# Third channel chunk of a dense convolution on TensorE: computed twice, or once and copied across partition halves

## The chip, the cores and the metric

The kernel runs on one core of one Trainium2 chip. The metric is the device time of one execution in microseconds (us). The core has five engines, each with its own queue: TensorE (PE, its weight loads shown as PEld), VectorE (DVE), ScalarE (ACT), GpSimd (POOL) and SyncE (SP, which here only issues DMAs). They work side by side and wait for each other through semaphores. TensorE writes its results into PSUM, eight banks of 128 partitions x 512 float32; ACT or DVE copy them out to SBUF. Such a copy is called an eviction here.

## The reference, cut to what matters

Eight sequences of 4160 tokens, 192 channels, eight heads of 24 channels. Each head has seven taps; they are put through a softmax and used as a causal convolution along the tokens. The result goes token by token into a maxout layer and an output product.

```python
w = softmax(weight)                                   # 8 heads x 7 taps
out = np.einsum('hk,bskhg->bshg', w, x_unf)           # y[s] = sum over k of w[h,k] * x[s - 6 + k]
x = out.reshape(B * S, D)                             # 33280 x 192
h = np.maximum(np.maximum(x @ w1, x @ w2), x @ w3)    # 192 -> 768
return (h @ w_out).astype(np.float32)                 # 768 -> 192
```

The kernel computes the maxout as max(relu(y(w1-w3)), y(w2-w3)) and adds y(w3 w_out) to the last product, so the third first-layer product is never made per token.

## The kernel before, in words

The tokens are worked on in 65 blocks of 512. The 192 channels are three chunks of 64. The first layer's operands have channels on partitions, 64 to a half, so that two 64-row products run on the two halves of the array: one half makes lp (w1-w3), the other lq (w2-w3). The convolved input therefore has to lie on both halves.

Blocks 4 to 64 get their convolution in token order (`conv`, L354), are transposed by DMA, and POOL copies them to the other half (`double`). The first four blocks, which open the kernel, use the dense conv (`conv_dense`, L376), which gives channels on partitions directly. It multiplies slots of 32 channels of x (tile xz, stationary, 32 columns wide) with a band matrix of the taps. A block is five chunks of at most 103 tokens; a slot of 32 channels can span two heads, so each product is made from two versions v of xz, which are added in PSUM. Four slots at a time go to four column groups of the array, that is to partitions 0, 32, 64 and 96 of the result.

For n = 0 these are slots 0 to 3, the first two channel chunks: PSUM tile D0, evicted to `yd[:, 0, :]`. `cross` (L395) copies each half of that to the other half. For n = 1 they are slots 4, 5, 4, 5: the third channel chunk made twice, once for each partition half, in PSUM tile D1, evicted in one copy to `yd[:, 2, :]`. In blocks 0 and 1 the crossing is done on the weights instead of the data (`cross_wd`, L322).

The order of the work is written out by hand: each engine runs its instructions in the order in which the program issues them. The steps around the change are, in this order (L692 to L741):

- `conv_dense(0)`: D0 evicted by ACT, D1 by DVE. Behind it: on ACT a zeroing of part of the input buffer of block 6 (`zero_x`, L140) and half of the casts of block 1 (`cast_dense`, L216); on DVE `copy_w3` (L316) and `make_wd` (L312). POOL makes the other half of the casts. The first-layer products of block 0 that need D0 (F) come on PE behind the conv.
- `conv_dense(1)` in the order n = 1, then n = 0: D1 evicted by ACT, D0 by DVE. On PE the products of block 0 that need its third chunk (H), then those of block 1 (H, F) in the pool psw, whose four buffers the four D tiles held before; these products of block 1 are the tiles lw. On DVE two `make_wd` and the first h of block 0.
- The rest of the first layer of blocks 0 and 1, a transposition of w3 on PE (`transpose_w3`, tiles pt), and the second layer of block 0 without its y part (`first_hidden`, L613).
- `conv_dense(2)`: D0 evicted by ACT, D1 by DVE, and then `cross` with ACT and DVE (L399). On PE `make_m` (L347), which multiplies w3 and w_out into the tiles pm0 and pm1; ACT evicts them (L349). Two zeroings (ACT L140, DVE L137). The pool psp, from which pm0, pm1 and then the lp of the main loop come, has two buffers.
- The main loop, block 2 first. It issues the first layer of a block (`l1`, L517) interleaved with the second layer of the block before (`st2`, L582); ACT makes r = relu(lp) (L500), DVE h = max(r, lq) (L505), ACT and DVE together add up two halves of the output (L589, L590).
- In block 2, behind its second first-layer tile, `conv_dense(3)`: D0 by ACT, D1 by DVE, a zeroing by DVE (L137), `cross` on POOL, the load and casts of later blocks.

SP's queue holds the loads of x and the stores and transposes, in program order. The loads of blocks 7 and 8 wait for zeroings of the buffers that they go to.

Of the kernel before, what the change touches and what calls it, by code (L numbers as in the profile page):

```python
# [19 lines left out]
GRP = 24  # L20
BAND_W = 128 + PAD
NBLK = 512
CHK = 103
HALF = P // 2
# [4 lines left out]
def kernel(  # L29
# [12 lines left out]
    nc = tc.nc  # L42
# [15 lines left out]
    for b in range(B):  # L58
        s = nfull * NBLK
        while s < SEQ:  # L60
            n = min(SEQ - s, NBLK - off)
# [13 lines left out]
    def conv_chunks(blk):  # L75
        res = []
        for (b, S, N, off) in blk:
            for o_lo in range(0, N, CHK):
                o_hi = min(o_lo + CHK, N)
                row_lo = max(0, S + o_lo - PAD)  # L80
                rlen = min(16 * ceil((CHK + PAD) / 16), SEQ - row_lo)
                res.append((len(res), b, row_lo, rlen, off + o_lo, off + o_hi,
                            o_lo - (row_lo - S)))
        return res

    NDENSE = 4
    chunks_of = [conv_chunks(blk) for blk in blocks[:NDENSE]]
    NQ = len(chunks_of[0])
# [42 lines left out]
    def zero_x(t, q0=0, q1=NR, eng=None):  # L131

        if t >= NDENSE:
            get_x(t)
        xf = xbuf[t]
        if eng is not None:
            eng.memset(xf[TOK:HALF, q0:q1, :], 0.0)  # L137
            return
        zero = idle[TOK:HALF, 0:D]
        nc.scalar.copy(out=xf[TOK:HALF, q0:q1, :],  # L140
                       in_=bass.AP(tensor=zero.tensor, offset=zero.offset,
                                   ap=[list(zero.ap[0]), [0, q1 - q0], [1, D]]))
# [43 lines left out]
    def cast_x(t):  # L186
        if not 0 <= t < NB:
            return
        xf, p0, _ = xin.pop(t)
        t0, u, nu = place(t)  # L190
        if u == 0:
            pool = x16q if nu >= 4 else x16p
            x16 = pool.tile([P, NHEAD * 4 * 2 * GRP * (5 if nu >= 4 else nu)], FP16, tag="x16", name=f"x16_{t0}")
            x16s[t0] = x16[:, 0:NHEAD * 4 * 2 * GRP * nu].rearrange("p (h j u r c) -> p h j u r c", h=NHEAD, j=4, u=nu, r=2)
        if p0:
            nc.gpsimd.memset(xf[0:p0, 0, :], 0.0)
        K = HALF + KR
        for r in range(2):
            nc.gpsimd.tensor_copy(out=x16s[t0][0:K, :, :, u, r, :].rearrange("p h j c -> p j h c"),  # L199
                                  in_=xf[0:K, 4 * r:4 * r + 4, :].rearrange("p j (h c) -> p j h c", c=GRP))  # L200
# [3 lines left out]
    xz = {t: [const.tile([P, NQ, D], FP16, name=f"xz_{t}_{v}") for v in range(2)] for t in range(2)}  # L204
# [72 lines left out]
    band = bands[:, 0:NHEAD * BAND_W].rearrange("p (h w) -> p h w", w=BAND_W)  # L277
# [11 lines left out]
    for lo, hi, copy in ((0, CUT, nc.scalar.copy), (CUT, WIN, nc.vector.tensor_copy)):  # L289
        bps = psq.tile([32, hi - lo + 3, NHEAD], FP32, tag="q", name=f"band_{lo}")  # L290
        for c in range(lo, hi):

            nc.tensor.matmul(bps[:, c - lo:c - lo + 4, :].rearrange("p c h -> p (c h)"),
                             lhsT=line[:, WIN - 1 - c:WIN + 31 - c],
                             rhs=ident16[:, 0:4 * NHEAD], start=True, stop=True)
        for a in range(4):
            copy(out=band[32 * a:32 * a + 32, :, 32 * a + lo:32 * a + hi],
                 in_=bps[:, 0:hi - lo, :].rearrange("p c h -> p h c"))
# [11 lines left out]
    def make_wd(n, j0, j1, eng=nc.vector):  # L310
        f = slice(P * j0, P * j1)
        eng.tensor_sub(out=wd[:, n, f], in0=ws[:, n, f], in1=w3s[:, n // 2, f])  # L312
# [5 lines left out]
    def cast_w3(j0, j1):  # L318
        f = slice(P * j0, P * j1)
        nc.gpsimd.tensor_copy(out=w3h[:, :, f], in_=w3s[:, :, f])  # L320
# [52 lines left out]
            slots[t0] = ysp.tile([P, 2, nu, 2, D], FP16, tag="ys", name=f"ys_{t}")  # L373
        convs[t0] = G, heads[0]

    def conv_dense(t, copies, pools=((None, None),) * 2, order=(0, 1)):  # L376


        yd = dense[t] = ydp.tile([P, NC, NBLK], FP16, tag="yd", name=f"yd_{t}")
        for n in order:  # L380
            slots_ = ((0, 1, 2, 3), (4, 5, 4, 5))[n]
            pool, tag = pools[n]
            ps = (pool or psw).tile([P, NBLK], FP32, tag=tag or "w", name=f"D{n}_{t}")
            for (q, b, row_lo, rlen, lo, hi, cc) in chunks_of[t]:
                for v in range(2):
                    for g, s in enumerate(slots_):
                        h = (32 * s + 31 * v) // GRP
                        nc.tensor.matmul(  # L388
                            ps[32 * g:32 * g + 32, lo:hi],
                            lhsT=xz[t][v][0:rlen, q, 32 * s:32 * s + 32],  # L390
                            rhs=band[0:rlen, h, cc:cc + hi - lo],
                            start=(v == 0), stop=(v == 1), tile_position=(0, 32 * g))
            copies[n](out=yd[:, 2 * n, :], in_=ps[:])

    def cross(t, *copies):  # L395

# [27 lines left out]
    def double(t):  # L424

        if not NDENSE <= t < NB:
            return
        yp = dense[t]
        for i in range(2):
            nc.gpsimd.tensor_copy(out=yp[HALF * i:HALF * (i + 1), 1, :, :, :, :].rearrange("p i u k n -> p (i u k n)"),  # L430
                                  in_=yp[HALF * (1 - i):HALF * (2 - i), 0, :, :, :, :].rearrange("p i u k n -> p (i u k n)"))
# [35 lines left out]
    def op(fn):  # L467
        ops.append((tuple(put), fn))
# [137 lines left out]
    def first_hidden(k):  # L606

        meet()
        first.append(psw.tile([P, 2, D], FP32, tag="w", name=f"po_0_{k}"))
        for s in range(2):  # L610
            for j in range(NJ):
                n = 2 * k + s
                nc.tensor.matmul(first[k][:, s, :], lhsT=hs[0][:, j, P * n:P * (n + 1)], rhs=wo[:, j, :],  # L613
                                 start=(s == 0 and j == 0), stop=False)
# [72 lines left out]
    PQ = ((psp, "p"), (psq, "q"))  # L687
    WW = ((psw, "w"), (psw, "w"))
    WPWQ = ((psw, "w"), (psp, "p"), (psw, "w"), (psq, "q"))
    ACT, DVE = nc.scalar.copy, nc.vector.tensor_copy  # L690
    GP = nc.gpsimd.tensor_copy
    make_wd(0, 0, 2)  # L692
    make_wd(1, 0, 2)
    zero_x(6, 4, NR, nc.vector)
    conv_dense(0, (ACT, DVE))
    zero_x(6, 0, 4)
    for t in range(NDENSE, XBUF):
        load_x(t)
# [7 lines left out]
    for n in range(NC):  # L706
        make_wd(n, 4, 6, nc.gpsimd)
    cast_w3(2, 6)
    conv_dense(1, (DVE, ACT), order=(1, 0))
    make_wd(0, 2, 4)  # L710
    make_wd(1, 2, 4)
    cross_wd(0, GP)
# [16 lines left out]
    cross_wd(1, ACT)  # L729
    first_hidden(0)  # L730
    first_hidden(1)
    conv_dense(2, (ACT, DVE), (WW[0], PQ[1]))
    cast_x(4)
    cross(2, ACT, DVE)
    make_m(0)
# [26 lines left out]
    for t in range(2, NB):  # L762
        u = convs_at.get(t, NB)
        late = t > 2 and u < NB
        if t in (3, 4):
            double(t + 1)
        if t > 3:
            for v in range(casts.get(t - 1, 8) + 1, casts[t] + 1):
                cast_x(v)
        l1(t, 0)  # L770
        if t == 2:
            first_rest()
        elif t == 3:
            cast_x(8)
            nc.gpsimd.tensor_copy(out=m16[0:HALF, 2, :], in_=m16[HALF:P, 0, :])
            nc.gpsimd.tensor_copy(out=m16[HALF:P, 2, :], in_=m16[HALF:P, 1, :])
        if t > 3 and not late:
            op(lambda t=t: (store(t - 2, 0, 4, (nc.sync,)),
                            turn(t + 2, (2,)) if place(t + 2)[1:] in ((0, 4), (0, 5)) else None,
                            turn(t + 1, (4,)) if place(t + 1)[1:] == (0, 5) else None, load_on(t)))  # L780
        else:
            op(lambda t=t: store(t - 2, 0, 4, (nc.sync,)))
        cuts = ROOM if late else EVEN
        st2(t - 1, (cuts[0], cuts[0]))
        for j in range(1, NJ):
            l1(t, j)
            if late and j == 1:
                st2(t - 1, (cuts[0] + OWN + AHEAD, cuts[0] + OWN))
                meet()
                quad, second = u >= QUADS, u < QUADS or t == u - 3  # L790
                conv(u, WPWQ, range(4 * second, 4 * second + 4) if quad else range(NHEAD))
                for i in (0, 2):
                    evac(u, i)
                for i in (1, 3):
                    evac(u, i, nc.vector.tensor_copy)
                if second:
                    turn(u)
                load_on(t)
            if t == 2 and j == 1:
                meet()  # L800
                conv_dense(3, (ACT, DVE))
                zero_x(1, NQ, NR, nc.vector)
                cross(3, GP, GP)
                load_x(8)
                cast_x(6)
            elif t == 2 and j == 3:
                meet()
                conv(u, WW)
                evac(u, 0)
                evac(u, 1, nc.vector.tensor_copy)  # L810
                turn(4)
                load_x(9)
                cast_x(7)
            st2(t - 1, (cuts[j], cuts[j]))
            if j == 1 and t > 4 and t + 2 in pairs and pairs[t + 2][1] % 2 == 0:
                double(t + 2)
            if t == NB - 1 and j == 3:
                op(lambda: store(NB - 2, 0, 2, (nc.sync,)))
        if t == NB - 1:
            op(lambda: store(NB - 2, 2, 4, (nc.sync,)))  # L820
# [29 lines left out]
```

## Time and profile before

| what | value |
|---|---|
| median of 3 runs | 453.1 us (452.54 to 453.47) |
| profiled execution | 452.5 us, span 450.7 us |
| PE busy | 444.7 us, 99% of the span |
| DVE / ACT / POOL busy | 356.5 / 320.3 / 204.0 us |
| DMA | 72.01 MB, mean 160 GB/s |
| dense conv matmuls (L388) | 320, from 6.2 to 27.2 us, 205 to 221 ns each, overlapping |
| evictions of D (L393) | 4 by ACT, 586 ns; 4 by DVE, 684 to 692 ns |

The span runs from the first to the last instruction of the profiled execution; all times in a timeline are us from its start. A line of the timeline gives the start, the duration, the engine, the line of the kernel, the operation, the output and input tiles with partitions x elements, how many instructions it merges, and in brackets the idle time of that engine just before and what ended it. The duration of a merged line runs from the first start to the last end. Matmuls overlap, so the sum of their durations is no time on the engine. In the groups by shape the columns behind the bar are the busy time in us, the mean duration in ns, and the idle time in front.

### The profile page before, as it was taken

What the parts mean: (1) busy time and instruction counts of PE and PEld (TensorE: products, weight loads), DVE (VectorE), ACT (ScalarE), POOL (GpSimd) and SP (SyncE); (2) the same over time, 40 slices, a digit from 0 to 9 for tenths busy, and PEclk for the clock granted to TensorE, in tenths of its full rate; (3) what the DMA queues carried; (4) which work ended last, traced back from release to release, by engine and by line L of the source; (5) the groups of instructions that cost most, each with busy time, mean ns of one, the idle gap of its engine ahead of it and who ended that gap; (6) DMA issues with size and microseconds to landing.
All of it is one profiled execution on the core that took longest, in us unless ns stands there. A gap on an engine that the chain in (4) does not pass through costs nothing.

```text
span 450.7 us, 18261 instructions
## 1 busy us (share of the span) xinstructions
PE 444.7 (99%) x7576; PEld 409.5 (91%) x7576; DVE 356.5 (79%) x610; ACT 320.3 (71%) x600; POOL 204.0 (45%) x234
## 2 busy tenths in 40 slices
PE   7999999999999999999999999999999999999997
PEld 4579999999999999999999999999999999999996
DVE  7778778878778787787887887887887887887775
ACT  7977677767677676776776777776776776776664
POOL 2874836556464524714724635526544545124000
PEclk9999999999999999999999999999999999999999
DMA  7978999495977759649559749769549566172123
GB/s 204 238 191 158 208 183 240 134 217 148 183 208 161 184 107 214 172 112 205 158 138 185 190 103 193 192 105 218 157 116 207 160 157 151 48 139 75 56 71 106
DMA packets 128242, 72.01 MB, mean 160 GB/s; under 512 B 52320, under 2 KB 127967, under 8 KB 128159
## 3 DMA queue, kind: packets, MB, share of 16 engines
q1 hardware_dynamic: 127999, 70.75, 68.8%
q8 instruction: 59, 0.97, 1.0%
q14 instruction: 24, 0.20, 0.2%
q10 hardware_dynamic: 160, 0.10, 0.1%
HBM read 33.28 MB, written 25.56 MB: 131 GB/s over the span
## 4 chain that ended last, share of the span: by engine, by line
PE 97%; DMA 1%; SPq 1%; issue 0%; DVE 0%; POOL 0%; POOLq 0%
PE po L582 36%; PE lq L517 32%; PE lp L517 22%; PE G L367 3%; PE lw L541 1%; DMA xf<-in_x_dram 1%; PE D L388 1%; PE lp L541 1%; PE po L613 0%; PE po L640 0%; SPq L233 0%; SPq L229 0%; PE pm L347 0%; PE lq L541 0%; SPq L167 0%; PE pt L338 0%
## 5 line engine op out<-in xcount | busy, mean ns | idle before, releaser
L582 PE MATMUL po<-wo,h 64*128 64x192 f16 x3024 | 331.7, 243 | 0.0
L505 DVE TENSOR_TENSOR h<-r,lq 128x512 f16<-128x512 f16 x384 | 263.0, 686 | 84.3 <-ACT r L500 74.3
L500 ACT ACTIVATE r<-lp 128x512 f16<-128x512 f32 x384 | 229.0, 597 | 113.4 <-PE lp L517 103.0
L517 PE MATMUL lp<-yp,wd 64*128 64x512 f16 x1098 | 295.6, 376 | 0.0
L517 PE MATMUL lq<-yp,wd 64*128 64x512 f16 x1098 | 295.5, 376 | 0.0
L582 PEld LDWEIGHTS <-h 64*128 64x128 f16 x3024 | 242.6, 94 | 5.5 <-issue 4.1
L517 PEld LDWEIGHTS <-wd 64*128 64x128 f16 x2268 | 181.6, 94 | 14.9 <-issue 0.2
L199 POOL CAST x<-xf 103x768 f16<-103x768 f32 x122 | 97.2, 825 | 112.4 <-DMA xf<-in_x_dram 108.9
L582 PE MATMUL po<-m,yp 64*128 64x192 f16 x720 | 140.3, 243 | 0.0
L430 POOL COPY yp<-yp 64x1536 f16<-64x1536 f16 (+1 forms) x70 | 90.9, 1298 | 87.3 <-DMA yp<-ys 62.3
L590 DVE TENSOR_TENSOR o<-a,po 128x384 f32<-128x384 f32 x126 | 69.0, 548 | 0.0
L582 PEld LDWEIGHTS <-yp 64*128 64x128 f16 x720 | 66.3, 94 | 0.1
L589 ACT COPY a<-po 128x384 f32<-128x384 f32 x126 | 59.5, 472 | 0.0
L407 ACT CAST ys<-G 128x480 f16<-128x480 f32 (+1 forms) x53 | 25.4, 530 | 9.5 <-PE G L367 9.5
L407 DVE CAST ys<-G 128x480 f16<-128x480 f32 (+1 forms) x53 | 30.2, 610 | 0.0
L367 PE MATMUL G<-x,band 39*32 39x240 f16 (+3 forms) x1024 | 16.5, 242 | 0.0
L367 PEld LDWEIGHTS <-band 39*32 39x32 f16 x1024 | 10.2, 91 | 4.6 <-issue 4.1
L517 PE MATMUL lq<-yd,wd 64*128 64x512 f16 x36 | 9.7, 376 | 0.0
L517 PE MATMUL lp<-yd,wd 64*128 64x512 f16 x36 | 9.7, 376 | 0.0
L541 PEld LDWEIGHTS <-wd 128*128 128x128 f16 (+1 forms) x48 | 3.1, 96 | 6.0 <-issue 2.8
L216 POOL CAST xz<-xf 112x160 f16<-112x160 f32 (+2 forms) x15 | 4.3, 330 | 7.9 <-DMA xf<-in_x_dram 7.8
L388 PEld LDWEIGHTS <-xz 112*32 112x32 f16 x320 | 3.9, 96 | 2.7 <-POOL xz L216 1.1
(79 smaller groups left out, 98.1 us busy)
## 6 DMA issues: line engine op xcount, KB each, us to landing
xf<-in_x_dram SPq DMA_DIRECT2D x113, 234.0 KB
out_dram<-o SPq DMA_DIRECT2D x62, 384.0 KB
wall<-in_moe_w_dram SPq DMA_DIRECT2D x12, 128.0 KB
xf<-in_x_dram SPq DMA_DIRECT2D x7, 204.8 KB
xf<-in_x_dram SPq DMA_DIRECT2D x3, 420.0 KB
yp<-ys SPq DMA_TRANSPOSE x70
out_dram<-o SPq DMA_DIRECT2D x5, 192.0 KB
wos<-in_moe_w_out_dram SPq DMA_DIRECT2D x1, 576.0 KB
```

The lines of the kernel that those rows point to most:

```text
L199: nc.gpsimd.tensor_copy(out=x16s[t0][0:K, :, :, u, r, :].rearrange("p h j c -> p j h c"), in_=xf[0:K, 4 * r:4 * r + 4, :].rearrange("p j ( ...
L367: nc.tensor.matmul(G[2 * (k // per) + i][TOK * j:TOK * (j + 1), k % per, :], lhsT=band[row, h, HALF * i + LAP:HALF * i + KR], rhs=x16s[t0] ...
L388: nc.tensor.matmul(ps[32 * g:32 * g + 32, lo:hi], lhsT=xz[t][v][0:rlen, q, 32 * s:32 * s + 32], rhs=band[0:rlen, h, cc:cc + hi - lo], star ...
L407: copy(out=slots[t][:, i % 2, :, :, GRP * h0:GRP * (h0 + per)].rearrange("p u r (h c) -> p h (u r) c", c=GRP), in_=G[i][:].rearrange("p h ...
L430: nc.gpsimd.tensor_copy(out=yp[HALF * i:HALF * (i + 1), 1, :, :, :, :].rearrange("p i u k n -> p (i u k n)"), in_=yp[HALF * (1 - i):HALF * ...
L500: nc.scalar.activation(out=r[:], in_=ps[0][:], func=AF.Relu)
L505: nc.vector.tensor_max(out=hs[t][:, j, :], in0=r[:], in1=q[:])
L517: nc.tensor.matmul(ps[i][:], lhsT=w_of(i, c, j), rhs=y_all(t, i, c), start=(n == 0), stop=(n == NC - 1))
L541: nc.tensor.matmul(open_ps[t, j, i][:], lhsT=a, rhs=b, start=(t, j, i) not in begun, stop=(t, j, i) in begun)
L582: nc.tensor.matmul(ps[b0, i][:, s % 2, :], lhsT=a, rhs=b, start=first, stop=last)
L589: nc.scalar.copy(out=a[:], in_=ps[s - 1, 0][:])
L590: nc.vector.tensor_add(out=outs[t][:, s - 1:s + 1, :], in0=a[:], in1=ps[s - 1, 1][:])
```

## The change

For n = 1 only two slots are multiplied per token chunk, 4 and 5, once. The five token chunks are dealt over the halves of the result: chunks 0, 1 and 2 (tokens 0 to 308) go to column groups 0 and 1 (partitions 0 to 63), chunks 3 and 4 (tokens 309 to 511) to groups 2 and 3 (partitions 64 to 127). They are issued in units of two token chunks, 0 with 3 and 1 with 4, and chunk 2 alone. The third chunk takes 20 matmuls instead of 40.

Each half of D1 then holds other tokens, and each has to reach both halves of `yd[:, 2, :]`. So the one eviction of 128 x 512 becomes four: tokens 0 to 308 of 64 partitions, to their own half and to the other one, by `copies[1]`, and tokens 309 to 511 in the same way by `copies[2]`. The argument `dup` would make the second copy from SBUF; no call gives it. Conv 0, 2 and 3 have DVE and ACT as these engines, conv 1 ACT and DVE.

```diff
-    def conv_dense(t, copies, pools=((None, None),) * 2, order=(0, 1)):
+    def conv_dense(t, copies, pools=((None, None),) * 2, order=(0, 1), dup=None):
         yd = dense[t] = ydp.tile([P, NC, NBLK], FP16, tag="yd", name=f"yd_{t}")
+        ch = chunks_of[t]
+        FAR = (NQ + 1) // 2
         for n in order:
-            slots_ = ((0, 1, 2, 3), (4, 5, 4, 5))[n]
+            if n == 0:
+                units = [[(c, 0, (0, 1, 2, 3))] for c in ch]
+            else:
+                units = [[(c, 2 * (c[0] // FAR), (4, 5)) for c in ch[k::FAR]] for k in range(FAR)]
             pool, tag = pools[n]
             ps = (pool or psw).tile([P, NBLK], FP32, tag=tag or "w", name=f"D{n}_{t}")
-            for (q, b, row_lo, rlen, lo, hi, cc) in chunks_of[t]:
+            for unit in units:
                 for v in range(2):
-                    for g, s in enumerate(slots_):
-                        h = (32 * s + 31 * v) // GRP
-                        nc.tensor.matmul(
...
+                    for (q, b, row_lo, rlen, lo, hi, cc), g0, slots_ in unit:
+                        for g, s in enumerate(slots_, g0):
+                            h = (32 * s + 31 * v) // GRP
+                            nc.tensor.matmul(
...
-            copies[n](out=yd[:, 2 * n, :], in_=ps[:])
+            if n == 0:
+                copies[0](out=yd[:, 0, :], in_=ps[:])
+            else:
+                far = ch[FAR][4]
+                for i, (lo, hi) in enumerate(((0, far), (far, NBLK))):
+                    own, other = (slice(HALF * k, HALF * (k + 1)) for k in (i, 1 - i))
+                    copies[1 + i](out=yd[own, 2, lo:hi], in_=ps[own, lo:hi])
+                    if dup is None:
+                        copies[1 + i](out=yd[other, 2, lo:hi], in_=ps[own, lo:hi])
+                    else:
+                        dup(out=yd[other, 2, lo:hi], in_=yd[own, 2, lo:hi])
...
-    conv_dense(0, (ACT, DVE))
+    conv_dense(0, (ACT, DVE, ACT))
...
-    conv_dense(1, (DVE, ACT), order=(1, 0))
+    conv_dense(1, (DVE, ACT, DVE), order=(1, 0))
...
-    conv_dense(2, (ACT, DVE), (WW[0], PQ[1]))
+    conv_dense(2, (ACT, DVE, ACT), (WW[0], PQ[1]))
...
-                conv_dense(3, (ACT, DVE))
+                conv_dense(3, (ACT, DVE, ACT))
```

More of the change, by code (lines that the diff above doesn't have):

```diff
@@ L382, in conv_dense @@
             pool, tag = pools[n]
             ps = (pool or psw).tile([P, NBLK], FP32, tag=tag or "w", name=f"D{n}_{t}")
-            for (q, b, row_lo, rlen, lo, hi, cc) in chunks_of[t]:
+            for unit in units:
                 for v in range(2):
-                    for g, s in enumerate(slots_):
-                        h = (32 * s + 31 * v) // GRP
[L388 to L392, printed above, removed]
@@ L393, in conv_dense @@
-            copies[n](out=yd[:, 2 * n, :], in_=ps[:])
+                    for (q, b, row_lo, rlen, lo, hi, cc), g0, slots_ in unit:
+                        for g, s in enumerate(slots_, g0):
+                            h = (32 * s + 31 * v) // GRP
+                            nc.tensor.matmul(
+                                ps[32 * g:32 * g + 32, lo:hi],
+                                lhsT=xz[t][v][0:rlen, q, 32 * s:32 * s + 32],
+                                rhs=band[0:rlen, h, cc:cc + hi - lo],
+                                start=(v == 0), stop=(v == 1), tile_position=(0, 32 * g))
```

## The prediction

> **What bounds the kernel now.** I read the page's busy table and the chain that ended last, then the timeline of the stretch in which the dense conv runs, engine by engine, and last the groups by shape for durations.
>
> ```profile
> PE 444.7 (99%) x7576; PEld 409.5 (91%) x7576; DVE 356.5 (79%) x610; ACT 320.3 (71%) x600; POOL 204.0 (45%) x234
> ...
> PE 97%; DMA 1%; SPq 1%; issue 0%; DVE 0%; POOL 0%; POOLq 0%
> ```
>
> TensorE is busy from end to end at a granted clock of 9 tenths or more, and 97% of the chain is its own. So from about 12 us on, what PE gains or loses reaches the end, unless a wait for ACT or DVE takes it up. The dense conv (L388) runs four times, all before 28 us: PE starts it at 6.22, 9.87, 21.61 and 26.34. I call them conv 0 to 3. Each is 80 matmuls in 1.10 us (1.30 in conv 1, which waits for its casts). First ACT around conv 2:
>
> ```profile
> 22.32 0.59 ACT L393 CAST yd<-D 128x512 f16<-128x512 f32 x1
> 22.93 0.62 ACT L399 COPY yd<-yd 64x512 f16<-64x512 f16 x1
> 23.46 0.71 ACT L349 CAST m<-pm 128x192 f16<-128x192 f32 x2
> 24.20 0.67 ACT L140 CAST xf<-idle 32x576 f32<-32x576 f16 x1
> 24.89 0.60 ACT L500 ACTIVATE r<-lp 128x512 f16<-128x512 f32 x1
> 25.39 0.47 ACT L629 COPY o<-po 128x384 f32<-128x384 f32 x1
> ```
>
> ACT has no gap here. PE in the same stretch:
>
> ```profile
> 21.61 1.10 PE L388 MATMUL D<-band,xz 112*32 112x103 f16 x80
> 22.65 1.16 PE L347 MATMUL pm<-wo,w3t 128*128 128x192 f16 x12
> 23.81 0.37 PE L517 MATMUL lp<-yd,wd 64*128 64x512 f16 x1
> ```
>
> Pool psp has two buffers and pm0 and pm1 hold them, so the first lp of block 2 takes pm0's and waits for ACT's eviction of it (L349). That ends at 23.46 + 0.31 = 23.77, and lp starts at 23.81: PE and ACT arrive together, with no slack.
>
> Conv 1, all engines:
>
> ```profile
> 10.75 0.59 ACT L393 CAST yd<-D 128x512 f16<-128x512 f32 x1 [0.54 <-PE D L388]
> ...
> 11.23 0.69 DVE L393 CAST yd<-D 128x512 f16<-128x512 f32 x1 [1.59 <-PE D L388]
> ...
> 12.27 1.19 PEld L541 LDWEIGHTS <-wd 128*128 128x128 f16 x7 [0.63 <-issue]
> ```
>
> The weight load at 12.27 stood idle 0.63 us, against 0.42 at this place of the next two rounds. The lw of block 1 in front of it takes D0's PSUM buffer, and DVE frees that at 11.23 + 0.69 = 11.92: DVE's eviction, not PE, sets this place.
>
> Conv 3, on DVE:
>
> ```profile
> 27.67 0.68 DVE L393 CAST yd<-D 128x512 f16<-128x512 f32 x1
> 28.53 0.54 DVE L137 MEMSET xf<- 32x576 f32 x1 [0.17 <-issue]
> 29.27 0.69 DVE L505 TENSOR_TENSOR h<-r,lq 128x512 f16<-128x512 f16 x1 [0.20 <-ACT r L500]
> 29.88 0.55 DVE L590 TENSOR_TENSOR o<-a,po 128x384 f32<-128x384 f32 x1
> ```
>
> L590 ends at 30.43 and frees a po buffer; PE's weight load at 30.48 has idled 0.19 for it. DVE's own idle time between its conv 3 eviction and there is only 0.17 + 0.20.
>
> Rows for the new shapes, by shape, on ACT, then DVE:
>
> ```profile
> L349 ACT CAST m<-pm 128x192 f16<-128x192 f32 x2 | 0.6, 313 | 0.1
> ...
> L629 ACT COPY o<-po 128x384 f32<-128x384 f32 x1 | 0.5, 473 | 0.0
> ```
>
> ```profile
> L629 DVE COPY o<-po 128x384 f32<-128x384 f32 x1 | 0.6, 552 | 0.0
> ```
>
> **The change, part by part.**
>
> *Matmuls.* Four 32-column matmuls on different column groups run beside each other: 80 in 1.03 to 1.10 us is 20 sets of 51 to 55 ns. The third chunk had 5 token chunks x 2 versions = 10 sets; it becomes units (chunks 0+3, 1+4, 2) x 2 versions = 6 sets, the last two half filled. Four sets less: 4 x 52 = 0.21 us per conv. If the cost goes by instruction, 20 x 13.4 ns = 0.27; if two token chunks don't run beside each other, 0. I take 0.21, as PE already runs four different right sides at once.
>
> *Evictions.* One 128x512 copy per conv (DVE 0.69; ACT 0.59 in conv 1) becomes two 64x309 on one engine and two 64x203 on the other. By the line through 313 ns at 192 elements and 473 at 384, ACT takes 0.32 for 203 and 0.41 for 309. DVE's 552 at 384 and 690 at 512 give 1.08 ns per element: 0.47 for 309, 0.36 for 203. Half the partitions shorten nothing: the 64x512 copies (L399) take 0.62 and 0.58. Bounds are the rows on either side: on ACT 0.31 to 0.47, on DVE 0.23 (32x80, L297) to 0.69.
>
> *How closely they follow.* Some neighbours on ACT overlap: 24.89 + 0.60 is 25.49, and the next starts at 25.39. Others don't: 22.32 + 0.59 = 22.91 and 22.93; the band copies out of PSUM into one quarter of the partitions after the other (L297, 0.334 each) take 1.02 for three. On DVE two L505 take 1.28 against 2 x 0.685, but the full-height eviction of 22.77 (0.69) and the copy across halves at 23.49 don't overlap. The new pieces change halves at each step, so I take the rows without overlap for both engines: 0.02 between pieces. [...]
>
> *Conv 0.* PE ends long before ACT (7.60) and DVE (8.17) evict; later it idles 0.91 for D0, unchanged, and then for the casts of block 1. Its 0.21 is hidden: 0. On ACT the two pieces delay the zeroing (8.21, L140) by 0.68, to 8.89 to 9.72. Behind it stand ACT's casts of block 1: at 9.74 instead of 9.44. DVE's third chunk ends at 9.13 for 8.86; copy_w3 and make_wd behind it end near 9.9 and first serve at 11.1: 0.
>
> *Conv 1.* PE's second unit needs ACT's second cast, ready at 10.41 instead of 10.11; five of six sets follow, so the third chunk ends near 10.8 (10.75 before) and D0's near 11.34 (11.23). ACT: 10.82 + 0.41 + 0.02 + 0.41 = 11.66, for lw at 11.62: 0.1 late. DVE, new here, takes two pieces to 11.49, and only then D0: 11.51 to 12.20 instead of 11.92. So lw is 0.28 late; behind D0 on DVE are two make_wd and the first h, all 0.28 later, and PE wants them in turn. POOL's wd, which held PE's weights 0.05 at 14.15, takes back 0.05. Loss 0.23. Ends: a gain of 0.2 if the casts are on time and DVE's pieces are at 0.31; a loss of 0.5 at 0.47 each.
>
> *Conv 2* (times before shifts). PE ends 0.21 sooner, pm too (23.60). DVE: 22.56 + 0.47 + 0.02 + 0.47 = 23.52, its crossing copy from 23.49 to 23.54: 0. ACT: D0 22.32 to 22.91, pieces 22.93 and 23.27, crossing copy 23.61 to 24.23, pm0 24.25 to 24.56. So lp starts at 24.61 for 23.81: loss 0.80, PE's 0.21 swallowed. Behind on ACT: pm1, the zeroing (24.80 to 25.47), r of block 2 (25.49; its lp is ready 25.42), L629, which frees the buffer that conv 3 wants 0.8 later too: all in time. SP's load of block 7 waits for that zeroing, 0.6 later, less than PE's own delay: 0. Ends: pieces hidden, a gain of 0.21; both at 0.47, a loss of 1.1.
>
> *Conv 3.* ACT idles 1.02 before 28.64, which covers its 0.68. DVE takes 0.96 for 0.69: the memset slides to 28.80, h from 29.27 to 29.36, L590 ends at 30.52. PE, 0.21 sooner, waits for it: loss 0.09 (ends: gain 0.2, loss 0.4). POOL's crossing copies wait for D0 alone, and SP's load of block 8, behind that memset (now 29.07), has its cast at 38.14; the transposes queued behind that load on SP start at 30.85, 0.6 after it, which covers 0.27. No DMA is added. After 31 us all is as before, shifted.
>
> *Sum.* 0 + 0.23 + 0.80 + 0.09 = +1.1 us on the profiled execution's 452.5 us (span 450.7, 1.8 around it): 453.6. That execution stands 0.6 below the median of 453.1, so I forecast 454.2 for the median.
>
> **The rivals.** (1) *ACT's pieces overlap*, by 0.10 as at 25.39. Then conv 0's casts start on time (9.44), conv 1 loses nothing, and in conv 2 the pieces start at 22.82 and 23.05, pm0 ends at 24.12, lp at 24.17: loss 0.36. With conv 3: +0.4, 453.5. For it: the crossing copy of 22.93 overlaps pm by 0.09 across halves. Against: L297's three.
> (2) *PE's time counts*: ACT's pieces come in front of pm0 for nothing. For it: the chain is 97% PE. Against: ACT's full row from 22.32 on. Conv 2 and 3 gain 0.21 each, conv 1 up to 0.2: 452.5 to 452.7; at 0.27 each 452.3. It needs lp before 23.81, and is faster by 0.2% only beyond 0.27 each, since conv 0 is hidden.
> (3) *Two token chunks don't run together*, so PE saves nothing. The third chunk of conv 1 ends at 11.0, and DVE's D0 at 12.4: +0.45; conv 2 the same 0.80, conv 3 0.2: 454.5.
>
> **How the numbers follow.** A measurement of this kernel can tell about 0.2%, 0.9 us (its runs lie 452.54 to 453.47). Chances: my sum 0.50, rival 1 0.20, rival 2 0.10, rival 3 0.10, something not seen 0.10. Slower (over 454.0): 0.30 of my sum, which lies only 0.2 above the bound, 0.08 of rival 3, 0.03 of rival 1, 0.06 unseen: 0.47. Faster (under 452.2): 0.03 of rival 2, 0.02 unseen: 0.05. Within: 0.48. The range is 452.7 to 455.2: from rival 2's less favourable end to my sum with each ACT and DVE piece at its upper row.
>
> **What would show it.** Right: L388 near 0.9 us in conv 2; ACT's L393-like pieces near 0.32 with gaps of 0.02; its casts of block 1 near 9.74; D0 of conv 1 evicted near 11.5; lp of block 2 at 24.6 plus 0.23, PE idle in front. Wrong: lp near 24.2 and casts at 9.44 (rival 1); lp at 23.6 (rival 2); L388 still 1.1 (rival 3). A piece far from its line, or a new wait after 31 us, would break the sum.

## The result, and the profile after

The changed kernel takes 458.47 us (median of 6 runs, 457.36 to 460.04) against 452.82 us before (6 runs, 452.47 to 455.06): 1.19% slower by the ratio of the means, 1.0119, with a 95% interval of 1.0091 to 1.0146. The forecast was 454.2. The profiled execution took 457.36 us with a span of 455.6, 4.9 more than the 450.7 before. From its page, the busy table and the shares of the chain that ended last:

```profile
PE 445.7 (98%) x7496; PEld 408.9 (90%) x7496; DVE 357.6 (78%) x615; ACT 322.4 (71%) x607; POOL 204.1 (45%) x234
...
PE 95%; DVE 2%; ACT 1%; issue 1%; ACTq 0%; DVEq 0%
```

The new copies add 2 us to ACT's busy time and 1 to DVE's, far less than 4.9. The chain shows more: DVE, ACT and "issue" now hold 4% of it, where they held nothing. The totals of the waits between 8 and 36 us name the new ones:

```profile
DVE yd L405 <- ACT yd L407: 2.9, 1, 2.9
ACT yd L405 <- DVE yd L407: 2.1, 2, 1.1
...
PE lp L533 <- ACT m L349: 1.7, 1, 1.7
```

L405 and L407 are the new pieces: L405 the copy to a half's own partitions, L407 that to the other half. The first piece of the engine that comes second waits for the other engine's last one. (Of DVE's 2.9 in conv 1 only the last 0.88 is this wait: D1 was complete by 11.84, when ACT began on it, and DVE started at 12.72.) Conv 2 on ACT, the timeline:

```profile
24.96 0.59 ACT L400 CAST yd<-D 128x512 f16<-128x512 f32 x1
26.26 0.32 ACT L405 CAST yd<-D 64x203 f16<-64x203 f32 x1 [0.71 <-PE pm L347]
26.59 0.33 ACT L407 CAST yd<-D 64x203 f16<-64x203 f32 x1
26.94 0.62 ACT L415 COPY yd<-yd 64x512 f16<-64x512 f16 x1
27.58 0.54 ACT L349 CAST m<-pm 128x192 f16<-128x192 f32 x2
```

and on DVE:

```profile
25.19 0.47 DVE L405 CAST yd<-D 64x309 f16<-64x309 f32 x1 [2.11 <-PE D L394]
25.70 0.47 DVE L407 CAST yd<-D 64x309 f16<-64x309 f32 x1
26.09 0.40 DVE L415 COPY yd<-yd 64x512 f16<-64x512 f16 x1
```

ACT is free at 25.55 and D1 complete before 25.19, yet ACT's first piece starts at 26.26, just after DVE's second piece ends at 25.70 + 0.47 = 26.17. The profile puts this idle time down to pm, which ended last by its clock (26.25); in conv 0 and 3, where no pm stands beside it, it names DVE's L407, and there too ACT starts 0.09 us after that piece ends:

```profile
9.21 0.32 ACT L405 CAST yd<-D 64x203 f16<-64x203 f32 x1 [1.01 <-DVE yd L407]
...
32.85 0.32 ACT L405 CAST yd<-D 64x203 f16<-64x203 f32 x1 [1.10 <-DVE yd L407]
```

Everything queued behind on ACT in conv 2 is late with the wait, and PE stands for the eviction of pm0:

```profile
24.23 0.92 PE L394 MATMUL D<-band,xz 112*32 112x103 f16 x60
25.08 1.17 PE L347 MATMUL pm<-wo,w3t 128*128 128x192 f16 x12
27.95 0.37 PE L533 MATMUL lp<-yd,wd 64*128 64x512 f16 x1 [1.71 <-ACT m L349]
```

The conv itself does what was meant: from its start to that of pm it is 0.85 us instead of 1.04.

Where the 4.9 us came from can be read at three marks on PE in the profiled executions: the start of conv 2, of the first lp of block 2, and of the convolution of block 7 (L367), which lies behind all four dense convs. "Own" is what a stretch adds to the mark before.

| mark | before | after | shift | own |
|---|---|---|---|---|
| conv 2 starts (conv 0 and 1 behind) | 21.61 | 24.23 | +2.62 | +2.62 |
| first lp of block 2 (conv 2) | 23.81 | 27.95 | +4.14 | +1.52 |
| convolution of block 7 (conv 3) | 42.46 | 47.36 | +4.90 | +0.76 |
| end | 450.7 | 455.6 | +4.9 | 0 |

### The profile page after: what moved, and what is told of

Read it like the earlier page. It is cut to its first block, busy times and chain, and to the rows that moved or that the text cites. A ratio compares the mean times of both kernels' runs of the same rounds, so it can differ in the third digit from the quotient of the medians.

```text
span 455.6 us, 18113 instructions
## 1 busy us (share of the span) xinstructions
PE 445.7 (98%) x7496; PEld 408.9 (90%) x7496; DVE 357.6 (78%) x615; ACT 322.4 (71%) x607; POOL 204.1 (45%) x234
## 4 chain that ended last, share of the span: by engine, by line
PE 95%; DVE 2%; ACT 1%; issue 1%; ACTq 0%; DVEq 0%
PE po L598 36%; PE lq L533 31%; PE lp L533 21%; PE G L367 3%; PE lw L557 1%; PE lp L557 1%; PE po L656 0%; PE po L629 0%; PE D L394 0%; ACT r L516 0%; PE pm L347 0%; ACT yd L407 0%; DVE yd L407 0%; ACT yd L405 0%; PE lq L557 0%
## 5 line engine op out<-in xcount | busy, mean ns | idle before, releaser
L367 PE MATMUL G<-x,band 39*32 39x240 f16 (+3 forms) x1024 | 16.5, 243 | 0.0
L367 PEld LDWEIGHTS <-band 39*32 39x32 f16 x1024 | 10.2, 92 | 4.6 <-issue 4.1
```

Of the source, the lines that this page charges most:

```text
L367: nc.tensor.matmul(G[2 * (k // per) + i][TOK * j:TOK * (j + 1), k % per, :], lhsT=band[row, h, HALF * i + LAP:HALF * i + KR], rhs=x16s[t0] ...
```

## The experiments

Theory A, formed from these waits: the two engines' pieces run one after the other, because both read the PSUM tile D1. Theory B: they wait because both write into the same result tile yd. Theory C: no wait is needed for the loss; the pieces' own time and the lower clock (PE's granted clock, shown below) make it. Each ratio below is of the means, against runs of the kernel before taken beside it: median 452.74 for two tiles, PE kept busy, conv 0 and conv 2; 453.2 for the other four.

**The two halves in two PSUM tiles.** The upper half's matmuls and copies use a second tile, E1; matmuls, pieces and engines are the same, and some tiles behind it come to lie in other buffers.

```diff
...
+            pt = [ps, ps]
+            if n == 1:
+                fp, ft = far_pool or (psw, "w")
+                pt[1] = fp.tile([P, NBLK], FP32, tag=ft, name=f"E1_{t}")
...
-                                ps[32 * g:32 * g + 32, lo:hi],
+                                pt[g // 2 if n else 0][32 * g:32 * g + 32, lo:hi],
...
-                    copies[1 + i](out=yd[own, 2, lo:hi], in_=ps[own, lo:hi])
+                    copies[1 + i](out=yd[own, 2, lo:hi], in_=pt[i][own, lo:hi])
...
-                        copies[1 + i](out=yd[other, 2, lo:hi], in_=ps[own, lo:hi])
+                        copies[1 + i](out=yd[other, 2, lo:hi], in_=pt[i][own, lo:hi])
...
-                conv_dense(3, (ACT, DVE, ACT))
+                conv_dense(3, (ACT, DVE, ACT), far_pool=PQ[1])
```

> The changed kernel, but the third chunk's two halves lie in two PSUM tiles, D1 and E1, instead of one. Pieces, engines and matmuls are the same. Theory A (the two engines' pieces run one after the other because they read the same PSUM tile): the idle of ACT before its pieces in conv 0 and 3 (1.01 and 1.10 us) and of DVE in conv 1 (2.95) goes, the first lp of block 2 follows pm by about 0.8 us less, and the time is that of the prediction's sum, about +1.1 over the kernel before: 453.5 to 454.5. Theory B (they wait because they write into the same result tile yd): nothing changes, 457.5 to 459. Theory C (the pieces' own time on ACT and DVE and the lower clock are the loss, not the wait): 457 or more.

454.11 us (5 runs), ratio 1.0043, interval 1.0027 to 1.006: about two thirds of the loss is gone (1.19% to 0.43% by the means, 4.9 to 1.6 us in the traces), with the same matmuls and the same copies by the same engines into the same yd. ACT in conv 2, from the timeline of this kernel:

```profile
23.05 0.59 ACT L404 CAST yd<-D 128x512 f16<-128x512 f32 x1
23.66 0.32 ACT L409 CAST yd<-E 64x203 f16<-64x203 f32 x1
24.00 0.33 ACT L411 CAST yd<-E 64x203 f16<-64x203 f32 x1
24.34 0.62 ACT L419 COPY yd<-yd 64x512 f16<-64x512 f16 x1
24.98 0.54 ACT L349 CAST m<-pm 128x192 f16<-128x192 f32 x2
25.55 0.67 ACT L140 CAST xf<-idle 32x576 f32<-32x576 f16 x1
```

There is no idle time in front of the pieces any more, and lp of block 2 starts at 25.36. The waits of ACT in conv 0 and 3 are gone too; DVE's idle time in conv 1 falls to 1.04, which is for the matmuls. Theory B falls, and so does theory C for the larger part of the loss: that part comes of the shared PSUM tile. The third that is left, 1.6 us in the trace, lies near the prediction's sum for the pieces alone, 1.1. The wait is in the program as it is built: in the changed kernel the second engine's first piece waits for the count that the first engine raises at its last piece; with two tiles it waits for PE alone. (The trace of the changed kernel has it as EVENT_SEMAPHORE at L405, three on ACT's queue and, in conv 1, one on DVE's.) The two engines read different halves of D1, and the program keeps them apart all the same. Each of these tiles is 128x512 float32, so the runs don't tell whether the wait goes by the tile or by some other piece of PSUM. No run reads the two halves of one tile at once, which would take the wait away alone; that the chip would allow it is not shown here.

**PE kept busy in front of conv 1.** In the changed kernel the granted clock falls to half for three microseconds. The stretches of one microsecond from 11 us (length, PE, PEld, DVE, ACT, POOL busy with instruction counts, then the clock, DMA share and GB/s):

```profile
11.00:12.00 1.00, 0.82 (x49) 0.69 (x53) 0.00 (x0) 0.67 (x4) 0.04 (x1) 0.94 0.91 216
12.00:13.00 1.00, 1.00 (x24) 0.40 (x15) 0.28 (x1) 0.67 (x2) 0.61 (x2) 0.50 0.94 194
13.00:14.00 1.00, 0.92 (x7) 0.13 (x4) 0.95 (x3) 0.94 (x2) 1.00 (x2) 0.50 0.64 177
14.00:15.00 1.00, 1.00 (x5) 0.13 (x2) 1.00 (x4) 0.15 (x1) 0.56 (x2) 0.50 1.05 354
```

```diff
+    keep_warm((NBLK,) * 8, psw, "w")
     conv_dense(1, (DVE, ACT, DVE), order=(1, 0))
```

> The changed kernel with eight more 512-column matmuls on zeros, whose result is used by nothing, on PE just in front of conv 1, where PE stands idle. Theory A (waits are the cause, the clock of 0.50 between 12 and 15 us a consequence of the idle time): the clock stays at 1.0, the conv and the products behind it take half the time, and about 0.8 us of the loss goes: 457 to 457.8. If the clock is the main cause: 454 to 455. If the clock doesn't follow from the idle time: the clock dips as before and the time is 458 or more.

458.57 us (4 runs), ratio 1.0133, 1.0112 to 1.0154: no better, a miss of theory A's number. The clock was 1.00 in all these stretches, so here the drop does follow from PE's idle time in front. But lw of block 1 started at 13.55, as in the changed kernel (13.54): both wait for DVE's last piece of the third chunk (L407, which ends at 13.49 and 13.48). The next first-layer tile of block 0 did start at 15.44 instead of 15.88; PE then waited 0.40 for h behind a make_wd on DVE that took 1.44 for 0.90, and conv 2 started at 24.52, not sooner than 24.23. The lower clock is a consequence here, and in the changed kernel what it costs on PE can be read as that 0.44, none of which is seen in the time.

**One conv at a time.** Four kernels, each with the new form in one conv and the old one in the others:

```diff
         FAR = (NQ + 1) // 2
+        DEALT = (0,)
...
-            else:
+            elif t not in DEALT:
+                units = [[(c, 0, (4, 5, 4, 5))] for c in ch]
+            else:
...
-            if n == 0:
-                copies[0](out=yd[:, 0, :], in_=ps[:])
+            if n == 0 or t not in DEALT:
+                copies[n](out=yd[:, 2 * n, :], in_=ps[:])
```

The others have (1,), (2,) or (3,) as DEALT.

> Only conv 0 in the new form, the other three as before. Theory A: ACT's two pieces wait for DVE's (1.0 us), the zeroing and the casts of block 1 behind them are 1.3 us late, conv 1 as well, and with the lower clock that follows the loss is 1.3 to 2.1 us: 454.1 to 454.9. Theory C (only the pieces' own time): the casts are 0.3 late, loss at most 0.4.

456.23 us, ratio 1.0096 (1.0064 to 1.0129); 455.02 in the profiled execution. More than either theory gave. ACT around conv 0:

```profile
7.60 0.58 ACT L403 CAST yd<-D 128x512 f16<-128x512 f32 x1
9.22 0.32 ACT L408 CAST yd<-D 64x203 f16<-64x203 f32 x1 [1.03 <-DVE yd L410]
9.55 0.32 ACT L410 CAST yd<-D 64x203 f16<-64x203 f32 x1
9.89 0.83 ACT L140 CAST xf<-idle 32x768 f32<-32x768 f16 x1
10.74 0.78 ACT L216 CAST xz<-xf 112x160 f16<-112x160 f32 x3
```

The wait is 1.03 us, and the casts of block 1 start at 10.74 for 9.44, as theory A said. PE stands at 11.12 for them, the clock then falls to 0.50 as above, the conv takes 1.77 us, and conv 2 starts 2.54 later than before. What of this is the lower clock no run separates.

> Only conv 1 in the new form. Theory A: DVE's two pieces wait for ACT's two and end near 12.15 us, so D0 of conv 1 behind them is evicted at 12.86 instead of 11.92, and the products of block 1 wait for it: loss 0.7 to 0.95 us, 453.5 to 453.7. Theory C (only the pieces' own time): 0 to 0.3 us.

455.27 us, ratio 1.0041 (1.0021 to 1.0062). DVE:

```profile
11.63 0.37 DVE L408 CAST yd<-D 64x203 f16<-64x203 f32 x1 [2.00 <-ACT yd L410]
12.01 0.37 DVE L410 CAST yd<-D 64x203 f16<-64x203 f32 x1
12.41 0.69 DVE L403 CAST yd<-D 128x512 f16<-128x512 f32 x1
```

D0 is evicted at 13.10 (expected 12.86, before 11.92), in an execution whose conv 1 began 0.19 late. Conv 2 starts 1.64 later; without the 0.19 the loss is 1.45, against 0.95 expected. What the expectation left out shows on DVE behind D0: the two make_wd there take 1.28 us together, against 0.75 before, and put off the first h by as much again. In the kernel before they are done at 12.59, as POOL's copy begins (12.56). In seven traces here they run beside POOL's copies or make_wd and take 0.90 to 1.44. In an eighth, that of the last experiment, they overlap by 0.36 and take 0.75, but POOL's copy takes 0.83 for 0.61. So DVE's late work also met POOL's here; whether POOL is the reason no run separates.

> Only conv 2 in the new form. Theory A: ACT waits for DVE's second piece to end, crossing copy and pm0 come 1.5 us later, and lp of block 2 too: loss 1.5 us, about 454.3. Theory C (only ACT's own pieces): 0.8 us, about 453.6.

455.89 us, ratio 1.0065 (1.0042 to 1.0088); 454.19 in the profiled execution. There the first lp of block 2 starts at 25.53, 1.72 after that of before, of which 0.20 was there when conv 2 started: 1.52 of its own, as theory A said and as in the changed kernel, not 0.8.

> Only conv 3 in the new form. Theory A: ACT's pieces wait for DVE's, r of the third first-layer tile of block 2 comes about 1 us late behind them, and PE, 0.2 us sooner at first, loses 0.9 at the output buffers: loss 0.7 us, about 453.4. Theory C: 0.1 us. If the single convs add up, the four give the 5.6 us of the changed kernel: 3.5 and 3.1 are measured for conv 0 and 2.

454.19 us, ratio 1.0029 (1.0013 to 1.0045). ACT waits 1.10 for DVE's L410, and of the shift of 1.14 at the convolution of block 7, 0.39 was there at the first lp of block 2: 0.75 of its own, as expected of theory A.

The single convs don't add up as the expectation supposed: by the marks they lose 2.54, 1.45, 1.52 and 0.75, together 6.3, against 4.9. Conv 0 and 1 lose 2.62 together, where conv 0 alone loses 2.54 and conv 1 alone 1.45; both delay the same products of block 1.

**All pieces on one engine.** One PSUM tile, as many pieces, but no second engine.

```diff
-    conv_dense(0, (ACT, DVE, ACT))
+    conv_dense(0, (ACT, DVE, DVE))
...
-    conv_dense(1, (DVE, ACT, DVE), order=(1, 0))
+    conv_dense(1, (DVE, ACT, ACT), order=(1, 0))
...
-    conv_dense(2, (ACT, DVE, ACT), (WW[0], PQ[1]))
+    conv_dense(2, (ACT, DVE, DVE), (WW[0], PQ[1]))
...
-                conv_dense(3, (ACT, DVE, ACT))
+                conv_dense(3, (ACT, DVE, DVE))
```

> The changed kernel with all four pieces of the third chunk on one engine: DVE in conv 0, 2 and 3, ACT in conv 1. The same number of copies, one PSUM tile, no second engine that could wait. Theory A: ACT's casts of block 1 and its pm0 are on time; what is left are the four pieces in a row, 1.7 us on DVE in conv 2 and 3 and 1.5 on ACT in conv 1: loss near 0 + 0.4 + 0.65 + 0.65 = 1.7 us, about 454.4. Theory C (the number of pieces is the loss): 457 or more, since one engine does all of them.

454.14 us, ratio 1.0027 (1.0015 to 1.0039), near the 454.4 expected; its trace loses 2.4 us, where 1.7 was expected. One engine alone was faster here than two that take turns (454.14 against 458.47): what hurt in the change was not the number of pieces, but that work of the other engine stood behind a wait. PE waits 0.21 at lp of block 2 and then 1.0 in conv 3, where DVE's four pieces take 29.19 to 30.91.

**Conv 3 alone, crossed by POOL.** Old form for conv 0 to 2 (DEALT = (3,) as above), and

```diff
-                conv_dense(3, (ACT, DVE, ACT))
+                conv_dense(3, (ACT, ACT, ACT), dup=GP)
```

> Conv 0, 1 and 2 as before; conv 3 with 60 matmuls, both halves evicted to their own half by ACT (0.41 + 0.32 us in an idle time of 1.02), and the two copies to the other half by POOL out of SBUF. DVE has no part of the third chunk. Theory A: PE's 0.2 us counts, since DVE's eviction of 0.69 in front of h is gone and nobody waits: 452.4 to 452.7, just faster or the same. If POOL's two copies in front of its casts are late for the convolution at 35 us: slower, 453 or more.

454.07 us (12 runs, 452.30 to 458.54) against 453.2 (30 runs, 452.21 to 455.5): ratio 1.002, interval 0.9997 to 1.0043, so no gain is shown, and a loss isn't either; the median missed the 452.4 to 452.7 expected. The trace shows what was expected in place: ACT's two pieces fit into its idle time, POOL's copies (27.95 to 28.80) hold up nothing, and the convolution of block 7 starts at 42.17 for 42.46; as this execution was 0.13 ahead at conv 2, conv 3 gains 0.16. That is 0.04%, below what a measurement of this kernel can tell. No version that beats the kernel before was found.

## Why the prediction was wrong, point by point

*The bound and the places.* The places named all counted: ACT's queue in front of pm0, DVE's eviction of D0 in conv 1, and L590 in conv 3 (there it was ACT's late r that held it up, not the length of DVE's own pieces). But the one that cost most alone, ACT's queue in front of the casts of block 1 in conv 0 (2.54), stands in the sum as 0; the prediction only carried 0.30 us of lateness over to conv 1. The direction was right, the size was not: +1.1 forecast, +4.9 in the traces and +5.65 in the medians.

*The matmuls.* Right: 0.21 forecast, 0.19 measured (1.04 to 0.85 from conv 2 to pm). Two token chunks on different column groups did run together, and rival 3 falls.

*The lengths of the pieces.* Right: forecast 0.32, 0.41, 0.47 and 0.36; measured 0.32, 0.41, 0.47 and 0.37.

*How closely they follow.* The choice of no overlap on one engine was right for ACT as well as for DVE, and rival 1 falls: in conv 2 the ACT pieces, the crossing copy and the pm eviction start 0.01 to 0.03 after the end of the one before, and DVE's second piece starts at 25.70, 0.04 after the end of its first (25.19 + 0.47). (On DVE the crossing copy at 26.09 did start 0.08 before its second piece ended.)

*The step that failed.* In each conv the prediction let the two engines copy their pieces at the same time: "ACT: D0 22.32 to 22.91, pieces 22.93 and 23.27" beside DVE's from 22.56, and in conv 1 DVE's two pieces beside ACT's. They take turns. The change adds a wait of one engine for the other, and the prediction listed none. In the kernel before no tile of PSUM is read by both ACT and DVE, so no row of its trace showed such a wait. With that wait taken away by two tiles, the prediction's own terms come out, but for a part of conv 1:

| step | forecast | changed kernel | two PSUM tiles |
|---|---|---|---|
| ACT's casts of block 1 start (conv 0) | 9.74 | 10.73 | 9.78 |
| D0 of conv 1 evicted from | 11.51 | 13.51 | 11.60 |
| conv 0 and 1 on PE, own | +0.23 | +2.62 | +0.71 |
| conv 2, own | +0.80 | +1.52 | +0.84 |
| conv 3, own | +0.09 | +0.76 | +0.10 |
| time | 454.2 | 458.47 | 454.11 |

In conv 2 the missing 0.72 is ACT's idle time of 0.71 in front of its pieces. In conv 3 the wait of 1.10 makes r late, and PE stands 0.33 and 0.58 for the two output buffers behind it (at 34.56 and 35.38), less the 0.19 that it had saved. In conv 0 and 1 the wait comes twice in a row, first ACT for DVE, then DVE for ACT. What the two-tile kernel still shows over the forecast there, 0.48, is for 0.34 a later start of its conv 1 (10.21 for 9.87), in an execution where POOL's casts came late (9.83 for 9.49). Part of the rest may be the two make_wd on DVE (1.16 for 0.75); it stays open.

*The two rivals left.* Rival 2 (PE's time counts) never came near, except in conv 3 once DVE was freed of its eviction. Rival 3 has fallen above. The case that came true was none of those listed, only the 0.10 of "something not seen": a wait that the change adds, which the working should have asked for at each new pair of instructions.

*After 31 us.* The profiled execution is shifted without a further loss (4.90 at 47 us, 4.9 at the end), as forecast. The difference of the medians is some 0.7 us above that of the traces, which is taken up below.

## What to carry to other kernels

Splitting one PSUM eviction over two engines made them take turns here as long as both halves lay in one PSUM tile: ACT idled 0.71 to 1.10 us for DVE's pieces and DVE 0.88 for ACT's, and what was queued behind the second engine was late with it. With the halves in two tiles these waits were gone, and even so it didn't pay (454.11 against 452.74). When a change lets a second engine touch a tile, ask first what the program will make it wait for, and then who stands behind it in its queue. The 0.19 us saved on PE in conv 2 were worth nothing in front of ACT's queue without a gap: even with two tiles this stretch lost 0.84. Count the queue's work before the matmuls'.

## What the runs showed of the hardware that was not expected

The granted clock fell after a short starvation. In the changed kernel PE was busy for 0.27, 0.42 and 0.82 of the microseconds from 9 to 12, and the clock was 0.50 from 12 to 15; with eight idle matmuls in the gap it stayed at 1.00. PE's longest pause between 7 and 12 us was 1.12 (7.13 to 8.25). In the same execution PE was busy for only 0.24 and 0.05 of the microseconds from 26 to 28, with a pause of 1.71, and the clock stayed at 1.00. What decides between the two no run here shows.

Several of the kernels here also scattered more than the kernel before, for a reason that the profile doesn't show. The profiled execution of the kernel with conv 3 alone in the new form took 457.16 us, where most of its runs took 453.5 to 455. Its timeline has this in a later convolution:

```profile
70.61 0.65 PE L367 MATMUL G<-x,band 39*32 39x96 f16 x57
73.02 0.23 PE L367 MATMUL G<-x,band 39*32 39x96 f16 x7 [1.75 <-issue]
```

PE stops after 57 of 64 matmuls for 1.75 us, "issue" being time in which it waits for nothing that the profile shows, and the clock is 0.50 from 74 to 76 us. The kernel with PE kept busy lost 1.20 in one piece in front of 66.31 us; there the profile names ACT's r, but that had ended at 65.33. What holds PE there stays open, and so does whether it is why single medians here lie up to 1.7 us above what their traces account for.
